# Linear attention and a two-layer FFN: one hand-assigned PSUM tile of eight banks, double-buffered attention in the first batches, weights held until v begins to land, constants cleared by GpSimd

## The chip, the cores and the metric

The kernel runs on one core of one Trainium2 chip. The metric is the device time of one execution in microseconds (us). Executions of one kernel vary by about 2 us here; a profile is of one execution, and its span is about 1.8 us shorter than the device time of the same run.

The engines are named as in the profile: PE (TensorE, matmuls; transposes are matmuls too), PEld (weight loads of PE, which overlap it), DVE (VectorE), ACT (ScalarE), POOL (GpSimd), SP (the queue that issues most DMAs). L128 is line 128 of the kernel file; line numbers differ a little between the kernels.

## The reference

```python
# q, k, v: [8 batches, 8 heads, 576, 64]; w_in [512, 2048], w_out [2048, 512], all fp32
theta = pi / 2 * arange(576) / 576
phi(x) = concat([relu(x) * cos(theta), relu(x) * sin(theta)], axis=-1)      # 128 features
kv  = einsum('bhsf,bhsd->bhfd', phi(k), v);  z = sum_s phi(k)
x   = (phi(q) @ kv) / (phi(q) . z + 1e-6)       # laid out as [4608 tokens, 512]
out = leaky_relu_0.01(x @ w_in) @ w_out         # fp32
```

The last output depends on everything, but the tokens can be done in groups. The kernel makes nine groups of 512 tokens; a batch has 576 tokens, so batch 0 and a part of batch 1 are needed before group 1 can start.

## The kernel before

A batch's 576 positions are five chunks: four of 128 and one of 64. Each chunk is prepared (relu times cos on ACT or DVE, relu times sin on DVE), its q is transposed on PE (`t_step`), multiplied with the batch's kv (`n_step`), divided, transposed again (`x_step`) and copied into `xT`. Then come the FFN's two layers, `ffn1` and `ffn2`. The banks of PSUM, into which PE's results go, are shared out among pools:

```python
psh_pool = ...(name="ps_h", bufs=2, space=PS)     # first layer
pso_pool = ...(name="ps_o", bufs=2, space=PS)     # second layer
psqt = ...(name="ps_qt", bufs=1, space=PS)        # q transposed
psnum = ...(name="ps_num", bufs=1, space=PS)      # numerators, two banks wide
pskx = ...(name="ps_kx", bufs=1, space=PS)        # kv, and x transposed
# ...
nc.vector.memset(vx[:, 0:J], 1.0)                 # v with a column of ones; twice, with
nc.vector.memset(t, 0.0)                          # the padded last chunks of k and q
# ...
gate(w1[0:1, 0, 0:1], main["q", 0][0:1, 0, 0, 0:1])   # weights' DMAs only after q has landed
```

```python
def n_step(b, c):
    pn = psnum.tile([P, 2, 512], dt.float32, name="pnum")
    # ... 8 matmuls (one a head) of kv with the transposed q, then on DVE:
    # den = pn's ones column + 1e-6;  rden = 1 / den;  xs = pn * rden
```

The prologue handles batch 0 with nothing else to do for PE. After it each group's period has 33 slots: 16 of `ffn1` (four matmuls each), 16 of `ffn2`, one more; attention for the next batch is hung into the slots. Group 0's period carries batch 1:

```python
for c in range(J):                       # the prologue
    prep("q", 0, c, "act")
    if c > 0:
        t_step(0, c - 1)
# ... v's casts (vcast), kv_mm(0, 0), kv_mm(0, 1)
for c in range(J + 1):
    if c < J: n_step(0, c)
    if c > 0: x_step(0, c - 1, "act")
# ...
if g == 0:                               # period of group 0
    for c in range(NCH):                 # NCH = 5, J = 4
        at(23 + c // 2, prep, "k", 1, c, "act")
        at(26 + c // 2, prep, "q", 1, c, "dve")
        at(28 + (c + 1) // 2, t_step, 1, c)
    at(31, vcast, 1, 0)                  # and two more casts, and both halves of kv
    for c in range(NCH + 1):
        if c < NCH: at(32, n_step, 1, c)
        if c > 0: at(32, x_step, 1, c - 1)
```

## Time and profile before

| | before |
|---|---|
| time, median of the first 3 runs | 348.26 us (347.99 to 349.23) |
| PE busy, of a span of 347.3 us | 311.5 us (90%) |
| DVE, ACT busy | 149.8, 160.3 us |
| first FFN matmul, and start of groups 1 and 2 | 33.04, 82.08 and 117.99 us (the chain of waits below has 118.16 for the last) |

The view of windows cut at those three starts gives, for each stretch, its length, each engine's busy time and (in brackets) instructions, the share of the TensorE clock that was granted, the DMA share and the GB/s.

```profile
core 0: us, PE busy (x) PEld busy (x) DVE busy (x) ACT busy (x) POOL busy (x), PEclk, DMA share, GB/s
0.00:33.04 33.04, 11.07 (x120) 9.00 (x121) 20.55 (x43) 11.43 (x18) 8.34 (x17) 1.00 1.07 219
33.04:82.08 49.04, 40.79 (x288) 21.99 (x288) 19.74 (x48) 21.03 (x32) 0.17 (x1) 0.89 0.83 215
82.08:117.99 35.91, 35.21 (x270) 18.61 (x269) 21.69 (x51) 16.89 (x27) 0.00 (x0) 0.96 0.27 70
117.99:347.30 229.31, 224.44 (x1599) 116.36 (x1596) 87.83 (x211) 111.00 (x171) 0.00 (x0) 1.00 0.36 96
```

The last stretch has PE busy for all but 4.9 us, which is the tail after the last matmul. What can be gained lies in the first two: 33 us with 11 us of PE work, and 49 us with 8 us of holes and a granted clock of 0.89. (PEclk reads 1.00 where no clock record exists. The first record starts at 37.2 us here, so the 1.00 of the first row says nothing of the clock: the first eight FFN matmuls, at 33.04 us, take 3.57 us, and eight take 1.73 us later.) Busy time alone would not say why PE is idle. The chain of waits does: it goes back from the end to whatever released each step. Here it is in order of time (start in us, length, what), for the prologue, with two lines of batch 1 at the end.

```profile
2.20 1.82 DVE vex L128
...
6.44 1.82 DVE vex L128
...
9.80 0.48 DVE qprem L134
10.29 1.47 DVE kp L173 x4
...
12.69 1.03 PE ps_qt L207 x8
13.74 0.70 DVE qpT L210
...
14.48 1.03 PE ps_qt L207 x8
...
26.22 0.63 PE pnum L219 x8
...
26.88 0.18 DVE den L225
...
27.08 0.21 DVE rden L229
...
27.32 0.70 DVE xs L231
...
28.06 0.64 PE pnum L219 x8
...
33.04 3.57 PE psh L263 x8
...
72.71 0.18 DVE den L225
...
74.56 0.18 DVE den L225
```

Three things are read from it. DVE clears constants for 8 us before it takes up k. One transpose bank makes PE and DVE take turns, 12.69 to 14.48 us: 1.79 us a chunk. One numerator buffer does the same with den, rden and xs, 26.22 to 28.06 us: 1.84 us a chunk. The hole before group 1 repeats this with batch 1: one den follows the other by 1.85 us there (72.71 and 74.56 us). The timeline (start, length, engine, line, what, and in brackets idle time before it and what ended that) shows batch 1's late k on ACT, v's casts far behind it, and the end of the hole:

```profile
57.68 2.93 ACT L165 ACTIVATE kp<-kmain,bias_zero,cos_t 128x512 f16<-128x512 f32 x4
...
68.12 1.28 DVE L182 CAST vex<-vmain 128x1024 f16<-128x1024 f32 x2
...
82.08 4.19 PE L263 MATMUL psh<-xT,w_136 128*128 128x512 f16 x12
```

Twelve first-layer matmuls take 4.19 us there; the chain has eight of them in 1.73 us when PE has been busy for a while, which would make 2.6 us for twelve. The Trainium skill, "TensorE: Matmul & The Clock Gate", Part 1, says that the clock is halved by default and after an idle window of about 3.4 us, and that those windows run free of the kernel. This trace agrees with the length: its clock records have 0.5 from 71.3 to 85.0 us, which is four times 3.4.

### The profile page before, as it was taken

Reading aid. Unit: us, or ns where it says so; the run is one execution under the profiler, and the core shown is the slowest. Engines: PE = TensorE matmul, PEld = TensorE weight load, DVE = VectorE, ACT = ScalarE, POOL = GpSimd, SP = SyncE. Lnnn points to the kernel's source line nnn. Section 1 sums busy time; section 2 is a strip of 40 time slices with the busy share of each in tenths; the row PEclk is TensorE's granted clock in tenths of the full one; section 3 lists DMA queues with packets and bytes.
Section 4 is the critical chain, followed back from the end, with each engine's and each line's share of the span. In section 5 each row is a group of like instructions: output and inputs, shape, how many; then the busy total and the mean of one; then the engine's idle time right before and its main releaser. Section 6 shows DMA issues by size and latency. Waiting matters only on the chain.

```text
span 347.3 us, 5458 instructions
## 1 busy us (share of the span) xinstructions
PE 311.5 (90%) x2272; PEld 166.0 (48%) x2272; DVE 149.8 (43%) x353; ACT 160.3 (46%) x247; POOL 8.5 (2%) x18
## 2 busy tenths in 40 slices
PE   0346999757999999999999999999999999999994
PEld 0243544443555555555555555555555544444441
DVE  6753340648268346715662577167525520000000
ACT  4502564142554464456355644564366217526711
POOL 0710000000000000000000000000000000000000
PEclk9999999966999999999999999999999999999999
DMA  7999997099202394239224923691110120021022
GB/s 232 234 204 203 271 283 209 30 256 232 90 0 52 75 281 126 61 124 287 62 60 110 306 56 72 185 267 40 57 37 2 30 62 30 0 72 51 0 60 62
DMA packets 47400, 42.29 MB, mean 122 GB/s; under 512 B 14096, under 2 KB 42768, under 8 KB 47376
## 3 DMA queue, kind: packets, MB, share of 16 engines
q1 hardware_dynamic: 43152, 37.76, 40.8%
q0 software_dynamic: 4224, 4.19, 7.4%
q8 instruction: 18, 0.29, 0.4%
q14 instruction: 6, 0.05, 0.0%
HBM read 36.70 MB, written 9.44 MB: 133 GB/s over the span
## 4 chain that ended last, share of the span: by engine, by line
PE 87%; DVE 10%; issue 1%; ACT 1%; POOL 0%; POOLq 0%; ACTq 0%; DVEq 0%
PE psh L263 36%; PE pso L293 35%; PE ps_qt L207 6%; PE pnum L219 4%; PE ps_kv L195 3%; PE ps_xt L243 2%; DVE xs L231 2%; DVE qpT L210 2%; DVE vex L128 1%; DVE vex L182 1%; DVE kp L173 1%; DVE rden L229 1%; DVE den L225 0%; ACT kv_sb L202 0%; DVE vex L186 0%
## 5 line engine op out<-in xcount | busy, mean ns | idle before, releaser
L263 PE MATMUL psh<-xT,w_136 128*128 128x512 f16 x576 | 139.2, 385 | 0.7 <-ACT xT L254 0.7
L293 PE MATMUL pso<-w_137,g 128*128 128x512 f16 x576 | 131.3, 379 | 0.0
L271 ACT ACTIVATE g<-psh,bias_zero 128x512 f16<-128x512 f32 x144 | 98.9, 687 | 60.2 <-PE psh L263 60.2
L293 PEld LDWEIGHTS <-g 128*128 128x128 f16 x576 | 54.5, 98 | 60.0
L263 PEld LDWEIGHTS <-w_136 128*128 128x128 f16 x576 | 53.9, 99 | 60.8 <-issue 10.2
L302 ACT COPY osb<-pso 128x512 f32<-128x512 f32 x36 | 21.1, 585 | 98.5 <-PE pso L293 72.6
L210 DVE COPY qpT<-ps_qt 128x1024 f16<-128x1024 f16 x40 | 27.7, 692 | 56.9 <-PE ps_qt L207 56.5
L207 PE MATMUL ps_qt<-ident,qp 128*128 128x128 f16 x256 | 21.1, 230 | 16.5 <-DVE qp L173 13.4
L231 DVE TENSOR_TENSOR xs<-pnum,rden 128x512 f16<-128x512 f32 x40 | 27.7, 692 | 1.4
L207 PEld LDWEIGHTS <-qp 128*128 128x128 f16 x256 | 17.3, 103 | 19.9 <-ACT qp L165 12.7
L165 ACT ACTIVATE kp<-kmain,bias_zero,cos_t 128x512 f16<-128x512 f32 x32 | 24.0, 806 | 3.8 <-DMA kmain<-in_k_dram 3.8
L225 DVE TENSOR_SCALAR den<-pnum 128x8 f32<-128x8 f32 x40 | 6.7, 167 | 43.1 <-PE pnum L219 43.1
L252 DVE COPY xT<-ps_xt 128x512 f16<-128x512 f16 (+1 forms) x40 | 14.4, 370 | 24.9 <-PE ps_xt L243 24.4
L219 PE MATMUL pnum<-kv_sb,qpT 128*128 128x66 f16 x320 | 18.9, 205 | 6.9 <-DVE xs L231 6.4
L219 PEld LDWEIGHTS <-qpT 128*128 128x128 f16 x320 | 16.4, 105 | 16.1 <-DVE xs L231 8.1
L243 PE MATMUL ps_xt<-ident,xs 128*128 128x128 f16 x160 | 17.5, 240 | 2.0 <-DVE xT L252 1.2
L243 PEld LDWEIGHTS <-xs 128*128 128x128 f16 x160 | 13.0, 107 | 9.8 <-DVE xT L252 1.5
L195 PEld LDWEIGHTS <-kp 128*128 128x128 f16 x256 | 12.3, 102 | 7.8 <-issue 4.9
L195 PE MATMUL ps_kv<-vex,kp 128*128 128x66 f16 x256 | 13.1, 200 | 2.8 <-DVE vex L182 1.9
L173 DVE TENSOR_SCALAR qp<-qmain,sin_t 128x512 f16<-128x512 f32 x32 | 15.6, 488 | 0.0
L173 DVE TENSOR_SCALAR kp<-kmain,sin_t 128x512 f16<-128x512 f32 x32 | 14.4, 472 | 0.7 <-DMA kmain<-in_k_dram 0.7
L169 DVE TENSOR_SCALAR qp<-qmain,cos_t 128x512 f16<-128x512 f32 x28 | 13.4, 477 | 2.0 <-DMA qmain<-in_q_dram 2.0
(37 smaller groups left out, 96.7 us busy)
## 6 DMA issues: line engine op xcount, KB each, us to landing
kmain<-in_k_dram SPq DMA_DIRECT2D x8, 1024.0 KB, 7.6
qmain<-in_q_dram SPq DMA_DIRECT2D x8, 1024.0 KB, 10.2
vmain<-in_v_dram SPq DMA_DIRECT2D x7, 1024.0 KB, 9.4
out_dram<-osb SPq DMA_DIRECT2D x40, 128.0 KB, 2.4
out_dram<-osb SPq DMA_DIRECT2D x16, 256.0 KB, 2.4
w_136<-in_moe_w_in_dram POOLq DMA_DIRECT2D x4, 512.0 KB, 8.2
w_137<-in_moe_w_out_dram POOLq DMA_DIRECT2D x4, 512.0 KB, 16.6
krem<-in_k_dram SPq DMA_DIRECT2D x8, 128.0 KB, 8.1
```

Of the source, the lines that this page charges most:

```text
L165: nc.scalar.activation(t[0:r, :, 0:D], src, AF.Relu, bias=bias_zero[0:r], scale=cos_t[0:r, c : c + 1])
L173: nc.vector.tensor_scalar(out=t[0:r, :, D:F], in0=src, scalar1=0.0, scalar2=sin_t[0:r, c : c + 1], op0=ALU.max, op1=ALU.mult,)
L195: nc.tensor.matmul(ps[:, hh, :], lhsT=kps[b, c][:, h, :], rhs=vex[b % 2][:, c, h, :], start=(c == 0), stop=(c == NCH - 1),)
L207: nc.tensor.transpose(ps[:, h, :], qps[b, c][:, h, :], ident)
L210: nc.vector.tensor_copy(t, ps)
L219: nc.tensor.matmul(pn[:, h // HH, (h % HH) * NE : (h % HH) * NE + NE], lhsT=qpTs[b, c][:, h, :], rhs=kvs[b][:, h, :],)
L231: nc.vector.tensor_tensor(out=xs.rearrange("p (a b) e -> p a b e", a=2), in0=pn[:, :, 0 : HH * NE].rearrange("p a (b e) -> p a b e", e=NE) ...
L243: nc.tensor.transpose(ps[:, kc, :], xss[b, c][:, 2 * kc : 2 * kc + 2, :], ident)
L263: nc.tensor.matmul(psh, lhsT=w1[:, c, m * P : (m + 1) * P], rhs=xts[g][:, c, :], start=(c == 0), stop=(c == NKC - 1),)
L271: nc.scalar.activation(gt, psh, AF.Prelu, bias=bias_zero, scale=1.0, alpha=0.01)
L293: nc.tensor.matmul(pso, lhsT=gs[g, m][:, tt * P : (tt + 1) * P], rhs=w2[:, m, :], start=(m == 0), stop=(m == NFT - 1),)
L302: nc.scalar.copy(osb, pso)
```

## The change

The intent is to let PE and the engines that empty PSUM work at once where PE has nothing else to do, to free DVE at the start, to give v's DMA precedence over the weights, and to prepare batch 1 earlier. All PSUM becomes one tile whose banks are assigned by hand, so that a step may use other banks in the prologue than later.

```diff
-    psh_pool = ...; pso_pool = ...; psqt = ...; psnum = ...; pskx = ...   # cut
+    ps = ps_pool.tile([P, 8, 512], dt.float32, name="ps")
+    HB = (0, 1); OB = (2, 3); NB_ = (4, 5); QB = 6; KB = 7                # cut to one line
@@ constants
-        nc.vector.memset(vx[:, 0:J], 1.0)
-        nc.vector.memset(vx[:, J], 0.0)
-        nc.vector.memset(vx[0:REM, J], 1.0)
+        nc.gpsimd.memset(vx[:, 0:J, :, D:NE], 1.0)
+        nc.gpsimd.memset(vx[REM:P, J], 0.0)
+        nc.gpsimd.memset(vx[0:REM, J, :, D:NE], 1.0)
-            nc.vector.memset(t, 0.0)
+            nc.gpsimd.memset(t[REM:P], 0.0)
@@ weights
-    gate(w1[0:1, 0, 0:1], main["q", 0][0:1, 0, 0, 0:1])
+    gate(w1[0:1, 0, 0:1], main["v", 0][0:1, 0, 0, 0:1])
@@ prologue (kv_mm, t_step, n_step and x_step take a bank as an argument)
-            t_step(0, c - 1)
-    t_step(0, J - 1)
+            t_step(0, c - 1, "act" if c % 2 else "dve", bank=(6, 2, 3)[c - 1])
+    t_step(0, J - 1, "dve", bank=7)
-    kv_mm(0, 0)
-    kv_mm(0, 1)
+    kv_mm(0, 0, bank=0)
+    kv_mm(0, 1, bank=1)
-    prep("q", 0, J, "dve")                  # moved to behind the loop below
-            n_step(0, c)
+            n_step(0, c, banks=((4, 5), (2, 3))[c % 2])
-            x_step(0, c - 1, "act")
+            x_step(0, c - 1, "act", bank=6 + c % 2)
+    prep("q", 0, J, "dve")
@@ period of group 0
-                at(23 + c // 2, prep, "k", 1, c, "act")
-                at(26 + c // 2, prep, "q", 1, c, "dve")
-                at(28 + (c + 1) // 2, t_step, 1, c)
-            at(31, vcast, ...); at(31, kv_mm, 1, 0); at(31, kv_mm, 1, 1)  # cut to one line
+                at(20 + c, prep, "k", 1, c, "act")
+                at(24 + c, prep, "q", 1, c, "act")
+                at(26 + c, t_step, 1, c)
+            at(29, vcast, ...); at(31, kv_mm, 1, 0); at(31, kv_mm, 1, 1, 6)
-            (five chunks)   at(32, n_step, 1, c)      at(32, x_step, 1, c - 1)
+            (four chunks)   at(32, n_step, 1, c, ((4, 5), (0, 1))[c % 2])
+                            at(32, x_step, 1, c - 1, "act", 6 + c % 2)
@@ period of group 1 (b = 2); batch 2's k and v were prepared in slot 32 of group 0 before
-            o = 5 if g == 1 else 0
+            o = 7 if g == 1 else 0
+            if g == 1:
+                at(2, n_step, 1, J); at(4, x_step, 1, J)       # the fifth chunk of batch 1
+                at(c, prep, "k", b, c, "act") for c in 0..4    # cut
+                at(5, vcast, b, part) for part in 0..2         # cut
             at(5 * c + 4 + o, n_step, b, c);  at(min(5 * c + 7 + o, 31), x_step, b, c)
```

From group 2 on, nothing changes but names.

More of the change, by code (lines that the diff above doesn't have):

```diff
@@ L58, with bank16 @@
     PS = bass.MemoryType.PSUM
-    psh_pool = ctx.enter_context(tc.tile_pool(name="ps_h", bufs=2, space=PS))
-    pso_pool = ctx.enter_context(tc.tile_pool(name="ps_o", bufs=2, space=PS))
-    psqt = ctx.enter_context(tc.tile_pool(name="ps_qt", bufs=1, space=PS))
-    psnum = ctx.enter_context(tc.tile_pool(name="ps_num", bufs=1, space=PS))
-    pskx = ctx.enter_context(tc.tile_pool(name="ps_kx", bufs=1, space=PS))
+    ps_pool = ctx.enter_context(tc.tile_pool(name="ps", bufs=1, space=PS))
+    ps = ps_pool.tile([P, 8, 512], dt.float32, name="ps")
+    HB = (0, 1)
+    OB = (2, 3)
+    NB_ = (4, 5)
+    QB = 6
+    KB = 7
+    def bank16(i, n):
+        return ps[:, i, :].bitcast(dt.float16)[:, 0:n]
     ctx.enter_context(tc.manual_schedule())
@@ L186, in vcast, with kv_mm @@
             nc.vector.tensor_copy(vex[b % 2][0:REM, J, :, 0:D], rem["v", b][0:REM])
-    def kv_mm(b, hg):
+    def kv_mm(b, hg, bank=KB):
         if hg == 0:
             kvs[b] = kvpool.tile([P, H, NE], dt.float16, name="kv_sb")
-        ps = pskx.tile([P, HH, NE], dt.float32, name="ps_kv", tag="kx")
+        pk = ps[:, bank, 0 : HH * NE].rearrange("p (h e) -> p h e", e=NE)
         for hh in range(HH):
@@ L195, in kv_mm @@
                 nc.tensor.matmul(
-                    ps[:, hh, :],
+                    pk[:, hh, :],
                     lhsT=kps[b, c][:, h, :],
@@ L201, in kv_mm, with t_step, n_step @@
                 )
-        nc.scalar.copy(kvs[b][:, hg * HH : (hg + 1) * HH, :], ps)
-    def t_step(b, c, evac="dve"):
-        ps = psqt.tile([P, H, P], dt.float16, name="ps_qt")
+        nc.scalar.copy(kvs[b][:, hg * HH : (hg + 1) * HH, :], pk)
+    def t_step(b, c, evac="dve", bank=QB):
+        pt = bank16(bank, H * P).rearrange("p (h n) -> p h n", n=P)
         for h in range(H):
-            nc.tensor.transpose(ps[:, h, :], qps[b, c][:, h, :], ident)
+            nc.tensor.transpose(pt[:, h, :], qps[b, c][:, h, :], ident)
         t = qptpool.tile([P, H, P], dt.float16, name="qpT")
         if evac == "dve":
-            nc.vector.tensor_copy(t, ps)
+            nc.vector.tensor_copy(t, pt)
         else:
-            nc.scalar.copy(t, ps)
+            nc.scalar.copy(t, pt)
         qpTs[b, c] = t
-    def n_step(b, c):
-        r = P if c < J else REM
-        pn = psnum.tile([P, 2, 512], dt.float32, name="pnum")
+    def n_step(b, c, banks=NB_):
+        pn = ps[:, banks[0] : banks[0] + 2, :]
         for h in range(H):
@@ L237, in n_step, with x_step @@
         xss[b, c] = xs
-    def x_step(b, c, evac="dve"):
+    def x_step(b, c, evac="dve", bank=KB):
         r = P if c < J else REM
-        ps = pskx.tile([P, NKC, P], dt.float16, name="ps_xt", tag="kx")
+        px = bank16(bank, NKC * P).rearrange("p (k n) -> p k n", n=P)
         for kc in range(NKC):
-            nc.tensor.transpose(ps[:, kc, :], xss[b, c][:, 2 * kc : 2 * kc + 2, :], ident)
+            nc.tensor.transpose(px[:, kc, :], xss[b, c][:, 2 * kc : 2 * kc + 2, :], ident)
         c0 = b * S + c * P
@@ L251, in x_step @@
             if evac == "dve":
-                nc.vector.tensor_copy(xts[g][:, :, pos_ : pos_ + n], ps[:, :, off : off + n])
+                nc.vector.tensor_copy(xts[g][:, :, pos_ : pos_ + n], px[:, :, off : off + n])
             else:
-                nc.scalar.copy(xts[g][:, :, pos_ : pos_ + n], ps[:, :, off : off + n])
+                nc.scalar.copy(xts[g][:, :, pos_ : pos_ + n], px[:, :, off : off + n])
             off += n
     gs = {}
-    psos = {}
     def ffn1(g, m):
-        psh = psh_pool.tile([P, GRP], dt.float32, name="psh")
+        psh = ps[:, HB[m % 2], :]
         for c in range(NKC):
@@ L288, in ffn2 @@
     def ffn2(g, tt, quarter):
-        if quarter == 0:
-            psos[g, tt] = pso_pool.tile([P, DM], dt.float32, name="pso")
-        pso = psos[g, tt]
+        pso = ps[:, OB[tt % 2], :]
         for m in range(quarter * 4, quarter * 4 + 4):
@@ L345, in period @@
             for c in range(NCH):
-                at(23 + c // 2, prep, "k", 1, c, "act")
-                at(26 + c // 2, prep, "q", 1, c, "dve")
-                at(28 + (c + 1) // 2, t_step, 1, c)
-            at(31, vcast, 1, 0)
-            at(31, vcast, 1, 1)
-            at(31, vcast, 1, 2)
+                at(20 + c, prep, "k", 1, c, "act")
+                at(24 + c, prep, "q", 1, c, "act")
+                at(26 + c, t_step, 1, c)
+            for part in range(3):
+                at(29, vcast, 1, part)
             at(31, kv_mm, 1, 0)
-            at(31, kv_mm, 1, 1)
-            for c in range(NCH + 1):
-                if c < NCH:
-                    at(32, n_step, 1, c)
+            at(31, kv_mm, 1, 1, 6)
+            for c in range(J + 1):
+                if c < J:
+                    at(32, n_step, 1, c, ((4, 5), (0, 1))[c % 2])
                 if c > 0:
-                    at(32, x_step, 1, c - 1)
+                    at(32, x_step, 1, c - 1, "act", 6 + c % 2)
         elif b < B:
-            o = 5 if g == 1 else 0
+            o = 7 if g == 1 else 0
             at(o, kv_mm, b, 0)
             at(o + 1, kv_mm, b, 1)
+            if g == 1:
+                at(2, n_step, 1, J)
+                at(4, x_step, 1, J)
+                for c in range(NCH):
+                    at(c, prep, "k", b, c, "act")
+                for part in range(3):
+                    at(5, vcast, b, part)
             for c in range(NCH):
@@ L370, in period @@
                 at((32 if name == "v" else 18) if g == 0 else 0, load_one, name, b + 1)
-            s0 = 16 if g else 32
-            st = 1 if g else 0
-            for part in range(3):
-                at(s0 + st * part, vcast, b + 1, part)
-            for c in range(NCH):
-                at(s0 + st * (3 + 2 * c), prep, "k", b + 1, c, "act")
+            if g > 0:
+                for part in range(3):
+                    at(16 + part, vcast, b + 1, part)
+                for c in range(NCH):
+                    at(19 + 2 * c, prep, "k", b + 1, c, "act")
         for s in range(33):
```

## The prediction

> **What bounds the kernel now.** PE is busy 311.5 of 347.3 us (first part of the page), and the table of windows has it saturated from 90 to 342 us: FFN matmuls with attention in between, no gap to fill. What is lost lies before that. In the chain of waits the first FFN matmul starts at 33.04 us and group 1's FFN at 82.08 us, after a hole from 61.5 us.
>
> 1. Prologue, to 33.04. DVE clears constants until 10.3 us (chain: vex 1.82 us twice, and smaller ones); q lands at 10.74 us anyway (DMA issues). Then one transpose bank is emptied by DVE alone, 1.79 us a chunk; then one numerator buffer: PE 0.63, den, rden and xs 1.15, a cycle of 1.84 us.
> 2. Batch 1's attention, 61.5 to 82.1: ACT reaches k's cos at 57.68 only, transposes serialize, v's casts follow them on DVE (68.1), the two kv halves share a bank, and five numerator cycles take 1.84 us each.
>
> After 118.16 us (start of group 2) nothing changes.
>
> **What the change does.**
>
> - Clears leave DVE (8 us) for GpSimd. As q's landing limits the start, this moves the first transpose only from 12.69 to about 11.6.
> - Four transpose banks, two emptied by ACT (about 1.0 us by its measured 0.59 for half the size): v's cast at about 17.2 instead of 19.7. Separate kv banks save about 0.5 more.
> - Two numerator buffers: the cycle falls from 1.84 to DVE's 1.15 to 1.2 us. First FFN matmul at about 28.0: 5 us earlier.
> - The weights' gate moves from q's to v's first landing (12.24): weights land about 1 us later than 18.0 to 37.0, batch 1's k at about 43, q 47.5, v 51.5. Nothing waits for them.
> - Batch 1's prep moves to slots 20 to 28 and q's cos to ACT: five transposes hide among second-layer matmuls, v is cast before the last one is emptied, kv starts at about 61.5 and ends at 62.8; only four chunks (the fifth goes into period 1) at 1.2 us. Group 1's FFN at about 69.3 instead of 82.1: 12.8 us earlier, of which 5 are the prologue's.
> - Given back in period 1 (36.1 us before): the fifth chunk's PE work 0.5; k's cos of batch 2, formerly in the hole, now alternates with the activations (0.73 + 0.69 = 1.42 us of ACT per 0.865 us slot, five slots), about 1.4 us of PE stall; at slot 31 numerator and x transpose of the last chunk now follow directly, so PE waits for DVE, 1.3 us. The cold restart stays: eight FFN matmuls took 3.57 us there against 1.73 later. The Trainium skill, "TensorE: Matmul & The Clock Gate", Part 1, says the clock halves after an idle window of about 3.4 us; the trace agrees (granted clock 0.50 from 75 to 85 us).
>
> The Trainium skill, "PSUM — Partial Sum Buffer", Terms, forbids two engines on one bank at once; the built program waits bank by bank, so one tile of eight banks costs no false waits.
>
> Net: 5 + 7.8 − 2.7 to 3 = about 10 us.
>
> **Predicted: 338 us, 334 to 341.5 (8 in 10). Faster by over 2%: 0.86; within: 0.13; slower: 0.01.**
>
> **Right if** the first FFN matmul is at 27 to 29 us, numerator cycles are about 1.2 us, group 1's FFN starts at 68 to 71, period 1 takes 38 to 39.5 us with PE waiting for the activation in slots 4 to 7 and for xs at its end, and group 2 starts at about 108. **Wrong if** weights land later than first used, GpSimd's clears run past 12 us or hold up DVE, ACT's order (casts behind output copies) delays batch 1's transposes, or waits between banks appear in the steady state.

## The result

The changed kernel took 338.33 us (median of 4 runs, 337.17 to 338.68) against 348.75 us for the kernel before beside it (347.99 to 349.26), 10.4 us less. The ratio is 0.970, with a 95% interval of 0.9665 to 0.9729. A ratio is the mean time of one kernel's fast runs over that of the other's of the same rounds, so it is not quite the ratio of the medians quoted here.

The same windows of the kernel after, cut at the same three events (columns as above):

```profile
0.00:27.91 27.91, 10.65 (x120) 9.02 (x121) 12.54 (x31) 13.46 (x20) 12.52 (x27) 1.00 1.05 220
27.91:69.11 41.20, 38.37 (x277) 20.32 (x277) 16.14 (x39) 23.22 (x37) 0.17 (x1) 0.97 0.97 243
69.11:107.15 38.04, 36.46 (x281) 19.33 (x280) 21.25 (x52) 20.73 (x33) 0.00 (x0) 0.95 0.42 109
107.15:336.50 229.35, 224.44 (x1599) 116.43 (x1596) 87.58 (x211) 110.43 (x170) 0.00 (x0) 1.00 0.36 96
```

By stretch, and by subtraction of the lengths: the prologue is 5.13 us shorter, group 0's period 7.84 us shorter, group 1's period 2.13 us longer, and the rest is the same to 0.04 us. The sum is −10.80 us, which is the difference of the spans (336.5 and 347.3). The equal last stretch also shows that one tile of eight banks brings no waits between banks: PE's busy time in it is 224.44 us in both, and the view of waits lists none of PE there, before or after.

The chain of waits in order of time, of the kernel after:

```profile
2.02 8.56 DMA qmain<-in_q_dram
...
11.47 1.05 PE ps L212 x8
...
12.54 1.01 ACT qpT L217
...
24.85 0.69 DVE xs L235
25.54 0.09 DVE den L229
...
25.65 0.21 DVE rden L233
...
25.89 0.70 DVE xs L235
...
27.91 3.57 PE ps L266 x8
...
61.54 1.44 PE ps L200 x40
...
65.91 0.08 DVE den L229
...
66.95 0.08 DVE den L229
...
106.17 0.70 DVE xs L235
...
106.92 0.40 PE ps L247 x4
```

The clears are gone from it, and the first thing on it is now q's DMA: 2.02 to 10.58 us. Xs follows den follows xs on DVE without PE between them, 24.85 to 25.89 us: 1.04 us a chunk. In batch 1 it is 1.04 us too (65.91 and 66.95 us), where it was 1.85. The last two lines are new and cost something: at the end of group 1's period PE waits for xs. Batch 1 in the timeline:

```profile
49.14 2.22 ACT L170 ACTIVATE kp<-kmain,bias_zero,cos_t 128x512 f16<-128x512 f32 x3
...
59.93 1.29 DVE L187 CAST vex<-vmain 128x1024 f16<-128x1024 f32 x2
...
69.11 4.71 PE L266 MATMUL ps<-xT,w_125 128*128 128x512 f16 x12 [0.46 <-ACT xT L258]
```

K is prepared 8.5 us earlier and v is cast 8.2 us earlier, of which 5.1 are the prologue's. The first twelve FFN matmuls of group 1 still run at the slow clock: the clock records have 0.5 from 66.3 to 73.1 us, two windows of 3.4 us where the kernel before had four. In the 3.41 us before them PE was busy for 1.72 us.

### The profile page after: what moved, and what is told of

Read it like the earlier page. It is cut to its first block, busy times and chain, and to the rows that moved or that the text cites. A ratio compares the mean times of both kernels' runs of the same rounds, so it can differ in the third digit from the quotient of the medians.

```text
span 336.5 us, 5463 instructions
## 1 busy us (share of the span) xinstructions
PE 309.9 (92%) x2272; PEld 165.1 (49%) x2272; DVE 137.5 (41%) x331; ACT 167.8 (50%) x259; POOL 12.7 (4%) x28
## 3 DMA queue, kind: packets, MB, share of 16 engines
q0 software_dynamic: 4224, 4.19, 7.7%
## 4 chain that ended last, share of the span: by engine, by line
PE 89%; DVE 3%; DMA 3%; ACT 2%; issue 1%; SPq 0%; ACTq 0%
PE ps L266 38%; PE ps L294 37%; PE ps L212 6%; PE ps L200 3%; PE ps L223 3%; PE ps L247 3%; DMA qmain<-in_q_dram 3%; DVE xs L235 1%; ACT g L274 1%; DVE rden L233 1%; DVE vex L187 0%; ACT qp L170 0%; DVE den L229 0%; ACT qpT L217 0%; ACT xT L258 0%
## 5 line engine op out<-in xcount | busy, mean ns | idle before, releaser
L266 PE MATMUL ps<-xT,w_125 128*128 128x512 f16 x576 | 140.0, 386 | 1.5 <-ACT xT L258 1.1
L294 PE MATMUL ps<-w_126,g 128*128 128x512 f16 x576 | 132.0, 379 | 0.0
L274 ACT ACTIVATE g<-ps,bias_zero 128x512 f16<-128x512 f32 x144 | 98.8, 687 | 52.8 <-PE ps L266 52.7
L303 ACT COPY osb<-ps 128x512 f32<-128x512 f32 x36 | 21.0, 585 | 93.2 <-PE ps L294 67.4
L215 DVE COPY qpT<-ps 128x1024 f16<-128x1024 f16 x38 | 26.2, 690 | 46.4 <-PE ps L212 46.1
L212 PE MATMUL ps<-ident,qp 128*128 128x128 f16 x256 | 20.8, 230 | 12.4 <-ACT qp L170 12.4
L235 DVE TENSOR_TENSOR xs<-ps,rden 128x512 f16<-128x512 f32 x40 | 27.6, 691 | 1.4
L247 PE MATMUL ps<-ident,xs 128*128 128x128 f16 x160 | 16.8, 232 | 4.6 <-DVE xs L235 4.2
L223 PE MATMUL ps<-kv_sb,qpT 128*128 128x66 f16 x320 | 17.7, 200 | 0.6 <-ACT kv_sb L207 0.6
L200 PE MATMUL ps<-vex,kp 128*128 128x66 f16 x256 | 12.8, 199 | 1.6 <-DVE vex L187 1.6
## 6 DMA issues: line engine op xcount, KB each, us to landing
qmain<-in_q_dram SPq DMA_DIRECT2D x8, 1024.0 KB, 10.2
```

The source lines that it names most:

```text
L200: nc.tensor.matmul(pk[:, hh, :], lhsT=kps[b, c][:, h, :], rhs=vex[b % 2][:, c, h, :], start=(c == 0), stop=(c == NCH - 1),)
L212: nc.tensor.transpose(pt[:, h, :], qps[b, c][:, h, :], ident)
L215: nc.vector.tensor_copy(t, pt)
L223: nc.tensor.matmul(pn[:, h // HH, (h % HH) * NE : (h % HH) * NE + NE], lhsT=qpTs[b, c][:, h, :], rhs=kvs[b][:, h, :],)
L235: nc.vector.tensor_tensor(out=xs.rearrange("p (a b) e -> p a b e", a=2), in0=pn[:, :, 0 : HH * NE].rearrange("p a (b e) -> p a b e", e=NE) ...
L247: nc.tensor.transpose(px[:, kc, :], xss[b, c][:, 2 * kc : 2 * kc + 2, :], ident)
```

## The experiments

Eleven runs were made after the result, each kernel beside runs of the kernel before on the same chip. All gave correct results. "First FFN matmul" and the starts of the groups are read from each run's trace. Because the windows of the clock run free, the profile of one kernel can hold a slow stretch of 3.4 us in one execution and of 6.8 in another (of the kernel after, mean clocks from 0.979 to 0.994); so times are compared by medians, and positions are compared with the length of the slow stretch in view.

The theory: the prologue gained from double-buffered numerators and from several transpose banks, and only 1.1 us from the clears, since q lands at about 10.7 us whatever DVE does; batch 1 gained from its slots and from the numerators; the held weights gained nothing; group 1's period gave back about 2 us through ACT's load and one wait for xs. The rivals: the 8 us of clears were the bottleneck; or holding the weights was what counted; or the clock alone explains the stretches.

### e1_clears_alone: only the clears moved

```diff
 # the kernel before
-        nc.vector.memset(vx[:, 0:J], 1.0)          # and the other three
+        nc.gpsimd.memset(vx[:, 0:J, :, D:NE], 1.0) # as in the change
```

> The kernel before, with only the clears of the constants moved to GpSimd and cut to what has to be cleared. My theory: q's landing limits the start, so of DVE's 8 us of clears only about 1.1 us lies on the chain; the first transpose moves from 12.7 to about 11.5 us, the first FFN matmul from 33.0 to about 31.9, the time falls by about 1.1 us (ratio to before about 0.997). Rival A: the clears were the prologue's bottleneck, and all or most of the 5.1 us that the prologue gained in the full change came from them: first FFN matmul at 28 to 29 us, time 4 to 5 us less (ratio about 0.987). Rival B: the clears cost nothing, first FFN matmul still at 33.0.

Measured: 348.00 us against 349.14, −1.1 us; ratio 0.9967 (0.9934 to 1.0000). In the profile the first transposes start at 11.06 us and the first FFN matmul at 31.44, which is 20.38 us later; in the kernel before it is 33.04 − 12.69 = 20.35 us later. So the clears shift the start and change nothing behind it. Q landed about 0.7 us earlier in this run (9.99 against 10.74 us), which is why the first FFN matmul comes 1.6 us earlier and not 1.1. At that time q was no longer what the start waited for: the chain goes through k's DMA, which landed at 6.59 us, and ACT's cosines of k, which end at 10.30. So two things stand close behind the clears, q's landing and ACT's work on k; which of them comes last differs from run to run (q in the kernel after, k in after_again). The theory holds in the trace: 8 us off a chain were worth little over 1 us, because other work arrived just behind the cleared stretch. The times alone do not show it, since their interval reaches from 0 to 2.3 us.

### e2_one_numerator_buffer: the second numerator buffer undone

```diff
 # the kernel after
-            n_step(0, c, banks=((4, 5), (2, 3))[c % 2])
+            n_step(0, c)
-                    at(32, n_step, 1, c, ((4, 5), (0, 1))[c % 2])
+                    at(32, n_step, 1, c)
```

> The kernel after, with the numerators of the prologue and of batch 1 all in banks 4 and 5, so not double-buffered. My theory: the cycle from one den to the next goes back from about 1.1 to 1.84 us, three cycles in the prologue and three in batch 1: first FFN matmul at about 30.1 instead of 27.9 us, group 1's FFN at about 73.7 instead of 69.1, time about 4.6 us above the kernel after (ratio to before about 0.983). Rival: with the other changes in place the second buffer is worth under 1 us, because PE or ACT (emptying the transposed x) would set the cycle anyway (ratio about 0.970 to 0.972).

Measured: 342.59 us against 349.14; ratio 0.982 (0.9792 to 0.9847). That is 4.3 us above the kernel after. In the chain, den follows den by 1.82 us again. The first FFN matmul is at 29.91, 2.0 us later with the same start of the transposes (11.48), and the stretch from group 0 to group 1 is 43.41 us instead of 41.20. Of the parts of the gain that a run took out, this is the largest. (The slow stretch of this profile is 10.2 us long, against 6.8 in the kernel after, so the longer hole also costs some clock.)

### e3_one_transpose_bank: the transpose banks undone

```diff
 # the kernel after
-            t_step(0, c - 1, "act" if c % 2 else "dve", bank=(6, 2, 3)[c - 1])
-    t_step(0, J - 1, "dve", bank=7)
+            t_step(0, c - 1)
+    t_step(0, J - 1)
```

> The kernel after, with the four transposes of the prologue in one bank, all emptied by DVE. My theory: the cycle of 1.79 us a chunk returns; started at 11.5 us the last is emptied at about 18.6 instead of 16.9, so the first FFN matmul comes at about 29.6 instead of 27.9 us and the time rises by about 1.7 us (ratio to before about 0.975). Rival: the wait for v's last landing (14.9 us) and its casts hide it, and the time rises by less than 0.5 us.

Measured: 338.80 us against 349.14; ratio 0.9708 (0.9681 to 0.9735), so only about 0.5 us above the kernel after, between the theory and the rival. From the first transpose to the first FFN matmul it took 28.80 − 11.27 = 17.53 us, against 27.91 − 11.47 = 16.44 in the kernel after: 1.1 us, not 1.7. The missing 0.6 us is in v's casts. Here they take 1.29 us for the two halves and 0.41 for the remainder; in the kernel after, where they come 1.5 us earlier, they take 1.69 and 0.60. What slows the earlier ones is the subject of e8.

### e5_old_slots_batch1: batch 1's slots undone

```diff
 # the kernel after
-                at(20 + c, prep, "k", 1, c, "act")
-                at(24 + c, prep, "q", 1, c, "act")
-                at(26 + c, t_step, 1, c)
+                at(23 + c // 2, prep, "k", 1, c, "act")
+                at(26 + c // 2, prep, "q", 1, c, "dve")
+                at(28 + (c + 1) // 2, t_step, 1, c)
-                at(29, vcast, 1, part)
+                at(31, vcast, 1, part)
```

> The kernel after, with batch 1's preparation of k and q, its transposes and v's casts back in their slots of before (and q's cos back on DVE); separate kv banks, double-buffered numerators and four chunks instead of five kept. My theory: the casts end about 3 us later, since transposes, their emptying and the casts line up behind ACT's late k; group 1's FFN at about 72.2 instead of 69.1, time up by about 3.1 us (ratio to before about 0.979). Rival: the hole of before came from the numerator cycles alone, and the slots are worth under 1 us.

Measured: 341.49 us against 349.14; ratio 0.9795 (0.9764 to 0.9826), 3.2 us above the kernel after. Group 0 to group 1 takes 71.25 − 27.49 = 43.76 us instead of 41.20. That is 2.6 us in the profile, which is of the fastest of the four runs, and 3.2 us by the medians; 3.1 were expected. The slots are worth that within what the clock's windows blur.

### e4_weights_after_q: the weights' gate undone

```diff
 # the kernel after
-    gate(w1[0:1, 0, 0:1], main["v", 0][0:1, 0, 0, 0:1])
+    gate(w1[0:1, 0, 0:1], main["q", 0][0:1, 0, 0, 0:1])
```

> The kernel after, with the weights' gate back on q's landing instead of v's. My theory: nothing waits for the weights, and v's landing does not suffer, since the weights' first packets come after v's halves anyway; the time stays within 0.3% of the kernel after (ratio to before 0.967 to 0.972). GpSimd then issues about 1.5 us earlier, so v's casts may run clear of it (0.69 and 0.41 us each) and the first FFN matmul come up to 0.5 us earlier. Rival: holding the weights protects v; without it v's second half and remainder land 1 us or more later than at 13.9 and 14.9 us, and the time rises by as much.

Measured: 337.87 us against 349.33; ratio 0.9671 (0.9657 to 0.9684), no slower than the kernel after. V's two halves and its remainder land at 11.90, 13.97 and 14.83 us, as in the kernel after (12.08, 13.92, 14.89). The first FFN matmul is at 27.29 us. So holding the weights protects nothing here; this part of the change has no gain, and perhaps a cost of a few tenths.

### after_again: the kernel after, as a measure for the next three

> The kernel after, unchanged, as the measure for the three runs beside it on the same chip: ratio to before about 0.970, first FFN matmul at 27.9 us, group 1's FFN at 69.1, group 2's at 107.3.

Measured: 338.34 us (337.07 to 339.24) against 349.29; ratio 0.9686 (0.9665 to 0.9706). First FFN matmul 27.59, groups 1 and 2 at 69.02 and 107.20 us.

### e6_k2_cos_on_dve: batch 2's k cosines on the other engine

```diff
 # the kernel after
-                    at(c, prep, "k", b, c, "act")
+                    at(c, prep, "k", b, c, "dve")
```

> The kernel after, with batch 2's five k cosines (slots 0 to 4 of period 1) on DVE instead of ACT. My theory: ACT's alternation of cosine and activation held PE up in slots 4 to 7 by about 1.4 us; DVE is idle just then and takes them in 0.4 us each; PE no longer waits for the activation there, group 2's FFN starts about 1.4 us earlier (105.9), time down by as much (ratio to before about 0.966). Rival: the delay of period 1 is the cold clock, which ACT's waits only fill; then the time stays within 0.3 us.

Measured: 338.90 us against 349.29; ratio 0.9696 (0.9675 to 0.9716): no gain. Neither theory fits well. ACT's stall did go: from group 1's start to batch 2's first kv matmul it took 77.66 − 67.99 = 9.67 us, against 79.58 − 69.11 = 10.47 in the kernel after, and about 0.3 of this 0.8 us is the clock (twelve FFN matmuls in 4.44 us, not 4.71). But DVE, with five more instructions ahead of v's casts, became the next to wait for. PE's waits in group 1's period, as the view of waits gives them for this run (total us, times, longest):

```profile
PE ps L247 <- DVE xs L235: 1.2, 1, 1.2
PE ps L200 <- DVE vex L191: 0.7, 1, 0.7
...
PE ps L212 <- DVE qp L178: 0.2, 1, 0.2
```

The second and third of these are new. ACT's stall is also smaller than the 1.4 us that was predicted: in the kernel after, eight FFN matmuls start at 76.31 us and would end at 78.04 with the 1.73 us that eight take, and the next starts at 78.72; that is 0.7 us.

### e7_last_numerator_earlier: the last numerator two slots earlier

```diff
 # the kernel after
-                at(5 * c + 4 + o, n_step, b, c)
+                at(min(5 * c + 4 + o, 29), n_step, b, c)
```

> The kernel after, with the numerator of batch 2's last chunk at slot 29 of period 1 instead of slot 31, where its x transpose stays. My theory: the wait of PE for xs at the end of period 1 (1.22 us in the trace) vanishes, group 2's FFN starts at about 106.1, time down by 1.2 us (ratio to before about 0.966). Rival: PE's wait reappears elsewhere (for the emptied xT or for the activation), and the time stays.

Measured: 336.54 us (335.47 to 337.81) against 349.29; ratio 0.9646 (0.9622 to 0.9669), 1.8 us less than the kernel after beside it. PE's waits in group 1's period, first in the kernel after:

```profile
PE ps L247 <- DVE xs L235: 1.2, 1, 1.2
PE ps L266 <- ACT xT L258: 0.5, 1, 0.5
PE ps L266 <- ACT g L274: 0.2, 1, 0.2
```

and in this run:

```profile
PE ps L266 <- ACT g L274: 0.5, 2, 0.2
PE ps L266 <- ACT xT L258: 0.5, 1, 0.5
```

The wait for xs is gone and group 1's period is 36.38 us instead of 38.04. Of these 1.66 us, 1.2 are the wait. The profile is of the fastest of the five runs (335.47 us). Its slow stretch was 3.4 us long, and 6.8 in the kernel after: the first twelve FFN matmuls took 4.33 us, not 4.71, which accounts for most of the rest.

### e8_w2_after_casts: the second weight matrix issued after v's casts

```diff
 # the kernel after: the four DMA issues of w2 are moved from the top to behind the prologue's casts
     for part in range(3):
         vcast(0, part)
+    gate(w2[0:1, 0, 0:1], vex[0][0:1, J, 0, 0:1])
+    (the four issues of w2)
```

> The kernel after, with GpSimd's issues of the second weight matrix held until v's three casts in the prologue are done. My theory: the casts ran slow (0.885 and 0.60 us against 0.687 and 0.41 in the kernel before) because they met GpSimd writing DMA descriptors; issued after them, the casts take 1.3 and 0.41 us again, and all that follows comes 0.5 us earlier; the weights' landings do not change, since their queue still has the first matrix to move until 25.9 us (ratio to before about 0.9685). Rival A: the casts are slow for another reason (DMA writes into SBUF), and stay slow. Rival B: the issues, now 19 to 22 us, slow den, reciprocal or xs instead, and nothing is gained.

Measured: 337.55 us against 349.29; ratio 0.9664 (0.9644 to 0.9685), 0.8 us less than the kernel after beside it, with intervals that overlap. The trace decides. In the timeline of the kernel after, GpSimd issues the second matrix while DVE casts v:

```profile
15.72 3.12 POOL L151 DMA_DIRECT2D w_126<-in_moe_w_out_dram  x4
...
16.85 1.69 DVE L187 CAST vex<-vmain 128x1024 f16<-128x1024 f32 x2
...
18.46 0.60 DVE L191 CAST vex<-vrem 64x512 f16<-64x512 f32 x1
```

In this run it does so afterwards:

```profile
17.14 1.28 DVE L184 CAST vex<-vmain 128x1024 f16<-128x1024 f32 x2
...
18.34 0.41 DVE L188 CAST vex<-vrem 64x512 f16<-64x512 f32 x1
...
19.29 2.97 POOL L318 DMA_DIRECT2D w<-in_moe_w_out_dram  x4 [0.30 <-POOL w L79]
```

The casts are back to 1.28 and 0.41 us, and from the first transpose to the first FFN matmul it takes 27.60 − 11.76 = 15.84 us instead of 16.44. The first den and its reciprocal, which now meet the issues' end (21.82 to 22.23 us), keep their 0.17 and 0.20 us, so rival B falls too. The last of the weights lands no later (37.45 us in both); the last quarter of the first matrix lands at 27.40 instead of 25.88 us, and PE waits for neither. The Trainium skill, "SBUF — State Buffer", section "Who interferes with whom", says that DVE's casts can enter a mode in which they need a port pair shared with GpSimd, and that GpSimd's writing of DMA descriptors needs it too. The runs agree that the two disturb each other; rival A, that DMA writes slow the casts, does not fit, since the DMA share over the casts is 1.24 in both runs. E4 fits too: there the issues end at 17.19 us, and of the casts that start at 16.84 only the first pair is a little slow (1.46 and 0.41 us).

### e10_numerator_and_w2: both edits that helped

> The kernel after, with the two edits that helped alone: the last numerator of period 1 at slot 29, and the second weights' issues after v's casts. My theory: they work in different stretches and add up: 1.2 to 1.6 us and 0.5 us, about 336.3 us (ratio to before about 0.963). Rival: the gains alone were the phase of the granted clock's windows in those runs, and together they give no more than one of them (ratio 0.965 or above).

The edit is that of e7 and that of e8 in one kernel. Measured: 336.71 us (334.93 to 337.09) against 349.33; ratio 0.9628 (0.9606 to 0.9650). First FFN matmul 27.41, group 2 at 103.81. The mean ratio is as the theory has it, but its interval overlaps with that of e7 alone; that the two add up is likely and not shown by the times.

### e11_batch1_earlier: a version aimed at what was left

```diff
 # the kernel after, with e8's edit, and in the period of group 0:
-                at(20 + c, prep, "k", 1, c, "act")
-                at(24 + c, prep, "q", 1, c, "act")
-                at(26 + c, t_step, 1, c)
+                at(16 + c, prep, "k", 1, c, "act")
+                at(19 + c, prep, "q", 1, c, "act")
+                at(21 + c, t_step, 1, c)
+                at(27 + c, prep, "k", 2, c, "act")     # was in slots 0 to 4 of group 1
-                at(29, vcast, 1, part)                 # kv at 31, n_step and x_step at 32
+                at(24, vcast, 1, part)                 # kv at 26
+                at(27 + c, n_step, 1, c, ((4, 5), (0, 1))[c % 2])     # c = 0 to 3
+                at(29 + c, x_step, 1, c, "act", 6 + c % 2)
 # v of batch 2 loaded at slot 25 instead of 32; in group 1: o = 5, v's casts of batch 2 at slot 3
```

> A further version: the second weights' issues after v's casts; batch 1's preparation, transposes, casts and kv four to five slots earlier in period 0, so that its numerators and x transposes fall between the last second-layer matmuls and not after them; batch 2's k prepared by ACT in slots 27 to 31 of period 0 instead of slots 0 to 4 of period 1; kv at slots 5 and 6. My theory: what is left to gain lies in the hole before group 1's FFN (about 4.5 us without PE work), in its cold clock (about 2 us for the first 12 matmuls) and in the two stalls of period 1 (0.7 and 1.2 us). k, q and v of batch 1 have landed at 42.4, 46.5 and 50.5 us, early enough. Group 1's FFN at about 65 instead of 69.1, at full clock; group 2's at about 99.5 to 100.5 instead of 107.2; time about 331 us (ratio to before about 0.949). Rival: the landings of q and v of batch 1 or ACT's queue hold the transposes up, PE stalls inside the second layer instead, and the gain is under 3 us (ratio above 0.960).

Measured: 331.83 us (331.56 to 331.97) against 349.33; ratio 0.9498 (0.9485 to 0.9511), as the theory expected to within a microsecond. Its windows, cut at the same events:

```profile
0.00:27.49 27.49, 10.65 (x120) 9.01 (x121) 12.51 (x31) 13.49 (x20) 12.61 (x28) 1.00 1.02 220
27.49:65.92 38.43, 36.93 (x276) 19.50 (x276) 17.78 (x42) 26.38 (x42) 0.17 (x1) 1.00 1.03 255
65.92:100.44 34.52, 34.23 (x280) 18.79 (x280) 19.76 (x47) 17.22 (x27) 0.00 (x0) 1.00 0.51 128
```

With batch 1's numerators between second-layer matmuls, this profile has no slow stretch on record from 31.3 to 328.3 us, where the kernel after had 0.97 and 0.95. (Before 31.3 us there is no record, and the first eight FFN matmuls take 3.57 us here too.) The times also spread over 0.4 us only, where those of the kernel after spread over 2. That the second follows from the first is not shown: the other three runs have a mean clock of 0.988 to 0.989, this one 0.998, and no trace of them is kept. Such a loss can lie in the prologue, as in the trace of after_again, which has 0.5 on record from 25.5 to 32.3 us. Nor does this run say what each of its several edits is worth. The 4.5 us of hole in the expectation is an overestimate, since the windows of the kernel after have PE idle for 2.8 us in all of group 0's stretch. Group 1's start came at 65.92 instead of the 65 expected, because ACT had an output copy and the last of batch 2's k (1.3 us together in the chain) ahead of the last copy into xT.

## Why the prediction was right

The time was predicted at 338 us and measured at 338.33, and the mechanism behind it is the one that the runs show. That the two numbers are only 0.3 us apart is partly luck, since terms that were off or missing cancelled. Point by point:

- First transposes at about 11.6 us, limited by q's landing: 11.47 in the trace, with q's DMA on the chain. E1 has 1.1 us for the clears by its medians, with an interval from 0 to 2.3. The prediction did not name ACT's cosines of k, which end just before q lands.
- Numerator cycle from 1.84 to 1.15 to 1.2 us: from den to den 1.05, 1.22 and 1.05 us. E2 gives its whole worth, 4.3 us.
- First FFN matmul at about 28.0: 27.91. Two errors met here. The casts started earlier than predicted (16.85, not 17.2) and ran slower by 0.6 us, which was not foreseen although the overlap with GpSimd's issues could be read from the trace before (15.60 to 18.60 us against casts at 17.2).
- Weights about 1 us later than 18.0 to 37.0 us: 18.31 to 37.45, only 0.3 to 0.5 later. The first gate had taken GpSimd 1.39 us in the kernel before and took 0.18 here. Nothing waited for them, as said; e4 shows that the hold gains nothing.
- Batch 1: kv from 61.5 to 62.8, group 1's FFN at 69.3: 61.37 to 62.97, and 69.11. E5 gives the slots' worth, 3.2 us.
- Given back in group 1's period, 2.7 to 3 us: 2.13 us. The mis-sized term is ACT's stall: predicted 1.4, measured 0.7. The estimate took ACT's 1.42 us per slot against a full-clock slot of 0.865 us for all five slots, while the first two or three slots ran at the slow clock and gave ACT time to catch up. The wait for xs was predicted at 1.3 and measured at 1.2; e7 removes it. With the fifth chunk's 0.5, the prediction's own terms add up to 3.2. Two more were not foreseen and nearly cancel: in the kernel before, PE waited 0.7 us in this period for DVE's q (until 86.97 us), and the kernel after has no such wait; and its first twelve FFN matmuls took 0.5 us more (4.71, not 4.19) at the slow clock. So 0.5 + 0.7 + 1.2 + 0.5 − 0.7 = 2.2, against 2.13 measured.
- Group 2 at about 108: 107.15.

Not isolated by a run: the two kv banks (estimated at 0.5 us in the prologue) and the moving of the fifth chunk into group 1's period. The parts that were isolated (e1 1.1, e2 4.3, e3 0.5, e5 3.2 us, each to within 1 to 1.5 us) add up to 9.1 of the 10.4 us; that the parts simply add was not tested. What of a slow stretch's length is chance and what is caused by a change was not settled either; it blurs single profiles by about 1 us.

## What to carry to other kernels

Before counting on cleared work, ask what arrives next: 8 us taken off an engine were worth about 1, because a DMA's landing and another engine's work came just behind. A second PSUM buffer pays where producer and consumer take turns with nothing else to do, and the gain is the producer's share of each turn. Where PE has holes, look for other PE work to lay between the dependent steps, as e11 did; in its profile that also left no slow stretch behind the prologue. And put work moved off one engine on another only after checking what stands behind it there, which e6 did not survive.

## What the Trainium skill lacked or had wrong

- "SBUF — State Buffer", "Who interferes with whom", says that whoever is second is blocked fully, for the whole instruction of the first. Here the casts next to GpSimd's DMA issues grew from 0.69 to 0.89 us (mean of two) and from 0.41 to 0.60, about 0.2 us each, while one issue takes 0.78 us, and four issues grew only from 2.97 to 3.12 us. So a cast was not held up for as long as a whole issue. The sizes that the section gives (DVE 6.8 times or GpSimd 1.5 times slower, by who came first) are larger than those here: 1.3 and 1.5 times for the casts, 1.05 times for the issues.
- "TensorE: Matmul & The Clock Gate", Part 1, has the windows of about 3.4 us and that they run free. The slow stretches of these runs were 3.4, 6.8, 10.2 and 13.7 us, which agrees. It ties the halved clock to an idle window. Here the clock halved after 3.41 us in which PE was busy for 1.78 us (kernel before, longest wait 0.6 us) and for 1.72 us (kernel after, longest wait 1.0 us). No run shows up to which share of work the clock is lost.
- The same part says that the number of slow matmuls varies from run to run, and puts the cost of warming up at under 1% of a typical kernel's span. It does not say that the times of a kernel with such a hole can fall into groups. Of the 25 runs of the kernel before beside the experiments, the five with a mean clock of 0.985 took 347.90 to 348.26 us and the twenty with 0.976 to 0.980 took 349.14 to 349.59: two groups 1.2 us apart. The kernel after spread over 2.2 us (337.07 to 339.24), e11 over 0.4 us. That slow windows cause the spread is inferred, since no run set their phase, and it does not explain all: the slowest run of the kernel after had a mean clock of 0.990, and two faster ones had 0.979.
- A single-element cast on GpSimd took 1.39 us in the kernel before (from 10.80 us) and 0.18 in the other runs; no run tested why. "Who interferes with whom" has a candidate: it lists DVE's tensor_scalar among the operations that can contend with GpSimd, and DVE ran those without a break from 10.21 to 12.94 us. But in e1 and e4 the cast began 0.03 us after DVE's and still took 0.18.
